# Attention scores: the second product of a split matmul reads k's low part where it was written, against a zero-padded copy of q's high part

## The chip, the cores and the metric

The kernel runs on one core of a Trainium2 chip. The metric is device time in microseconds (us): the time of one execution from launch to end. The core's engines are TensorE (PE: matmuls, and PEld for its weight loads), VectorE (DVE), ScalarE (ACT), GpSimd (POOL) and SyncE (SP), which here only issues transfers (DMA). Each engine runs its own list of instructions in order; semaphores hold an instruction until what it needs is there. Matmul results go to PSUM, and VectorE or ScalarE must read them out before that PSUM buffer can be used again.

## The reference, cut to what matters

Three stages follow one another on inputs of batch 4 and sequence 768: a linear attention over 8 heads, a gated feed-forward layer, and a causal softmax attention over 4 "experts" with head size 64. Only the last one is touched:

```python
for e in range(E):                      # E = 4
    q = x @ wq[e]                       # [768, 384] @ [384, 64]
    k = x @ wk[e]
    v = x @ wv[e]
    scores = scale * (q @ k.transpose(0, 2, 1))
    scores = np.where(causal, -1000000000.0, scores)
    scores = scores - scores.max(-1, keepdims=True)
    a = np.exp(scores)
    a /= a.sum(-1, keepdims=True) + 1e-09
    ye = a @ v @ wo[e]
    ...                                 # weighted by the gate, summed into out
```

The weights wq and wk are large here, so the scores need more precision than one matmul in the short float format fp32r gives. Each of q and k is therefore kept as a high part (qh, kh, rounded to fp32r) and a low part (ql, kl, the rest).

## The kernel before

**Stages.** The linear attention and the feed-forward layer run interleaved in an order written out by hand until about 358 us of the span. The softmax attention follows, as class Attention. Its instructions are created by `run` in an interleaved order, and a list scheduler with a model of its own then sets each engine's order at build time; SyncE's transfers go through one queue in order.

**Pairs and units.** The attention works on 8 pairs of heads (2 for each of 4 batches), called pair 0 to pair 7 below. For each pair `qk_group` makes q and k for both heads at once (128 partitions, head 0 on partitions 0 to 63, head 1 on 64 to 127) in two halves of 384 columns: nine matmuls into a PSUM tile m, ScalarE writes the high part, VectorE writes the low part from m and the high part. The tiles m come from a pool of two buffers that `qk_group`, `v_group` (the values, nine matmuls of 260 columns each, six times per batch), `av` and `proj_out` share. `soft` makes scores for one head and one block of 128 rows of q (12 blocks per pair, 96 in all): two matmuls into a PSUM tile st (two buffers; for the two widest blocks two matmuls on each of two column halves, so 128 of each kind in all), then VectorE adds the mask and takes the row extreme (sm, mn), then ScalarE takes the exponential (A). `transp` scales A, transposes it in blocks of 128 and copies it to T; `av` multiplies by the values; `proj_out` projects and stores.

**The two products.** Both have all 128 partitions as the contraction, so a head's 64 rows are there twice. Tile sq holds qh of the head on its own 64 partitions and ql of the head on the other 64; tile sk holds kh on both. So the first product, sq with sk, is qh·kh + ql·kh. Tile sl holds kl on both halves, and the second product, sq with sl, is qh·kl + ql·kl. [...] The first product is called S1 and the second S2 below. In `soft` before:

```python
q = hl["sq"][j]
for i, k in enumerate((hl["sk"][j], hl["sl"][j])):
    nc.tensor.matmul(st[:, z, 0:n], q[:, qi * C:(qi + 1) * C], k[:, z * n:(z + 1) * n], start=(i == 0), stop=(i == 1))
```

**Where the two stages meet.** The attention's left pools (qh, ql, kh, kl, m and the weights) are open while the feed-forward stage still ends, so q and k of pair 0 are made there. The right pools (A, T, V, and the pool lp, which holds sl) take the memory that the feed-forward stage gives back, some of it only when the last weight (st_wo) has been split into its high and low parts by VectorE.

Of the kernel before, what the change touches and what calls it, by code (L numbers as in the profile page):

```python
# [47 lines left out]
DIAG_ON_ACT = 6  # L48
STEPS = (2, 1, 1, 1, 1, 1, 1, 1, 1, 1, 1, 1, 1, 0)
FROM = 8  # L50


def _f(ap):
# [852 lines left out]


class Attention:
    def __init__(self, tc, nc, a, x2, out, ident):
        self.tc, self.nc, self.a, self.x2, self.out, self.ident = tc, nc, a, x2, out, ident  # L910
        self.left, self.right = ExitStack(), ExitStack()
        self.flip, self.raw = True, {}

    def open_left(self):
        tc, nc, a = self.tc, self.nc, self.a
# [20 lines left out]
    def open_right(self):  # L936
        tc = self.tc
        R = lambda n, b, **k: self.right.enter_context(tc.tile_pool(name=n, bufs=b, side="right", **k))
        self.ap = R("ap", 2)
        self.sp = R("sp", 3)  # L940
        self.lp = R("lp", 2)
        self.ps_s = R("ps2_s", 2, space=PSUM)

    P3 = ((0, 0), (0, 1), (1, 0))
# [56 lines left out]
    def qk_group(self, xs, hl, n, p, h):  # L1001
        nc = self.nc
        w, sc = (self.wq, -0.125) if n == "q" else (self.wk, 1.0)
        if h == 0:
            hl[n] = [self.qp.tile([128, S], F32R, name=n + z, bufs=1) for z in "hl"]
        hi, lo = hl[n]
        s = slice(h * HT, (h + 1) * HT)
        pt = self.ps_m.tile([128, 512], F32, name="m")
        m = 0
        for i in range(3):  # L1010
            for wi, xi in self.P3:
                self.shown = nc.tensor.matmul(pt[:, 0:HT], w[wi][:, i, p * 128:(p + 1) * 128], xs[xi][:, i, s],
                                              start=(m == 0), stop=(m == 8))
                m += 1
        nc.scalar.activation(hi[:, s], pt[:, 0:HT], AF.Copy, scale=sc)
        nc.vector.scalar_tensor_tensor(lo[:, s], pt[:, 0:HT], sc, _f(hi[:, s]), op0=OP.mult, op1=OP.subtract)
        if h == 0:
            return
        ts = []
        for j in range(2):  # L1020
            o, z = slice(64 * j, 64 * j + 64), slice(64 - 64 * j, 128 - 64 * j)
            t = self.qp.tile([128, S], F32R, name=f"s{n}{j}")
            nc.sync.dma_start(_f(t[o]), _f(hi[o]))
            nc.sync.dma_start(_f(t[z]), _f((lo if n == "q" else hi)[o]))
            ts.append(t)
        hl["s" + n] = ts
        if n == "k":
            hl["sl"] = []
            for j in range(2):
                o, z = slice(64 * j, 64 * j + 64), slice(64 - 64 * j, 128 - 64 * j)  # L1030
                t = self.lp.tile([128, S], F32R, name=f"sl{j}")
                nc.sync.dma_start(_f(t[o]), _f(lo[o]))
                nc.sync.dma_start(_f(t[z]), _f(lo[o]))
                hl["sl"].append(t)

    def v_group(self, xs, V, t):
        nc = self.nc
        pt = self.ps_m.tile([128, 512], F32, name="m")
        m = 0
        for i in range(3):  # L1040
            for xi, wi in self.P3:
                nc.tensor.matmul(pt[:, 0:260], xs[xi][:, i, t * C:(t + 1) * C], self.wv[wi][:, i],
                                 start=(m == 0), stop=(m == 8))
                m += 1
        if t in V_ON_DVE:
            nc.vector.tensor_copy(V[:, t], pt[:, 0:260])
        else:
            nc.scalar.activation(V[:, t], pt[:, 0:260], AF.Copy)
# [27 lines left out]
    def soft(self, hl, j, qi, A, rs):  # L1076

        nc, sp = self.nc, self.sp
        W = (qi + 1) * C
        nb = 1 if W <= 512 else 2  # L1080
        n = max(W, 256) // nb
        q = hl["sq"][j]
        st = self.ps_s.tile([128, 2, 512], F32, name="st")
        for z in range(nb):
            for i, k in enumerate((hl["sk"][j], hl["sl"][j])):
                nc.tensor.matmul(st[:, z, 0:n], q[:, qi * C:(qi + 1) * C], k[:, z * n:(z + 1) * n], start=(i == 0),  # L1086
                                 stop=(i == 1))
# [12 lines left out]
        nc.scalar.activation(at, o3, AF.Exp, bias=mn, scale=-1.0, accum_out=rs[:, qi % 3:qi % 3 + 1])  # L1100
# [7 lines left out]
    def transp(self, A, rs, T, qi):  # L1108
        nc = self.nc
        q = qi % 3  # L1110
        at = A[:, self.OFF[qi]:self.OFF[qi] + (qi + 1) * C]
        if self.unit >= SCALED_ON_POOL:
            nc.gpsimd.tensor_tensor(at, at, rs[:, q:q + 1].to_broadcast([128, (qi + 1) * C]), op=OP.mult)
        else:
            nc.vector.tensor_scalar(at, at, rs[:, q:q + 1], None, op0=OP.mult)
        for k0 in range(0, qi + 1, 4):
            k1 = min(qi + 1, k0 + 4)
            pt = self.ps_t.tile([128, 4, C], F32, name="t")
            for ki in range(k0, k1):
                nc.tensor.transpose(pt[:, ki - k0], at[:, ki * C:(ki + 1) * C], self.ident)  # L1120
            self.flip = not self.flip
            to = T[:, k0:k1, q * C:(q + 1) * C]
            if self.flip:
                nc.scalar.activation(to, pt[:, 0:k1 - k0], AF.Copy)  # L1124
            else:
                nc.vector.tensor_copy(to, pt[:, 0:k1 - k0])  # L1126

    def av(self, Ts, V, p, h, O):
        nc = self.nc
        po = self.ps_m.tile([128, 512], F32, name="m")  # L1130
        n = 3 * (h + 1)
        for ki in range(n):
            lo = max(0, ki - 3 * h) * C
            for j in range(2):
                o = slice(64 * j, 64 * j + 64)
                nc.tensor.matmul(po[o, lo:HT], V[:, ki, (2 * p + j) * 64:(2 * p + j + 1) * 64], Ts[j][:, ki, lo:],  # L1136
                                 start=(ki == 0), stop=(ki == n - 1))
        s = slice(h * HT, (h + 1) * HT)
        nc.scalar.activation(O[0][:, p, s], po[:, 0:HT], AF.Copy)
        nc.vector.tensor_tensor(O[1][:, p, s], po[:, 0:HT], _f(O[0][:, p, s]), op=OP.subtract)  # L1140

    def proj_out(self, b, O, t):
# [2 lines left out]
        m = 0  # L1145
        for p in range(2):
            for oi, wi in self.P3:
                nc.tensor.matmul(pt[:, 0:DM], O[oi][:, p, t * C:(t + 1) * C], self.wo[wi][:, p], start=(m == 0),  # L1148
                                 stop=(m == 5))
# [8 lines left out]
    def run(self):  # L1158
# [26 lines left out]
        def softs(j):  # L1185
# [3 lines left out]
            for e in range(2):  # L1189
                for q in range(3):  # L1190
                    def f(e=e, q=q):
                        if q == 0:
                            A = ap.tile([128, (6, 15)[h] * C], F32, name=f"A{h}", bufs=3)
                            rs = sp.tile([128, 3], F32, name="rs", bufs=6)
                            st[j].append((A, rs))
                        if j % 4 == 1 and (e, q) == (1, 0):
                            with self.tc.issue_after(self.shown.ins):
                                self.soft(HL[i], e, 3 * h + q, *st[j][e])
                        else:
# [4 lines left out]
        def tail(j):  # L1204
# [4 lines left out]
            for e in range(2):  # L1209
                for q in range(3):  # L1210
                    def f(e=e, q=q):
# [5 lines left out]
                        self.transp(A, rs, Ts[e], 3 * h + q)  # L1217
                    todo.append(f)

            def g():  # L1220
                if b not in OS:
                    OS[b] = [ap.tile([128, 2, S], F32R, name=f"O{z}", bufs=1) for z in range(2)]
                self.av(Ts, VS[b], p, h, OS[b])
            todo.append(g)
            half[b, h] = half.get((b, h), 0) + 1
            if half[b, h] == 2:
                for t in range(3):
                    todo.append(lambda t=t: self.proj_out(b, OS[b], 3 * h + t))
            return todo

        st, half = {}, {}
# [35 lines left out]
def stages(tc, nc, a, x2, out, ident, stat, lim, top):  # L1267

    right = ExitStack()
    at = Attention(tc, nc, a, x2, out, ident)  # L1270
    mi = []

    def left2():
# [100 lines left out]
```

## Time and profile before

| what | value |
|---|---|
| median of 3 runs | 597.36 us (596.36 to 597.47) |
| the profiled execution: its time, its span from first to last instruction | 596.38 us, 594.7 us |
| share of the span that PE, DVE, ACT, POOL are busy | 95%, 83%, 67%, 29% |
| mean granted clock of TensorE over the span | 0.976 |
| the attention's stretch, 357.8 us to the end: PE busy | 225.4 of 236.9 us |

How to read it: a busy share is an average over stages with different limits. A matmul's record covers its way through the array, which overlaps the next matmul's start, so the start of one to the start of the next is shorter than a record (18 matmuls of 384 columns with records of about 0.345 us stand in 3.35 us), and a PE that waits shows less idle time than it lost: about 0.17 us less for each wait. A granted clock of 1.00 is 2.4 GHz, of 0.50 is 1.2 GHz.

### The profile page before, as it was taken

The numbers are of one execution on the slowest core, as the hardware profiler recorded it, in microseconds if no ns is written. First come the engines' busy times: TensorE is split into PE (matmuls) and PEld (weight loads), VectorE is DVE, ScalarE is ACT, GpSimd is POOL, SyncE is SP. The second block draws the span as 40 slices with busy tenths as digits, with TensorE's granted clock in tenths as the row PEclk, the third lists the DMA queues.
The fourth block names the chain that finished last, engine by engine and source line by source line (L and its number), as shares of the span: only waits on it lengthen the run. The fifth ranks groups of instructions, "written<-read, shape, count | busy, mean of one in ns | idle before, by whom it ended". The sixth has DMA issues, their size and how long they took to land. (4 is left out here: it accounts for less than half of the span.)

```text
span 594.7 us, 12388 instructions
## 1 busy us (share of the span) xinstructions
PE 563.1 (95%) x4386; PEld 507.1 (85%) x4386; DVE 493.5 (83%) x1153; ACT 398.0 (67%) x1015; POOL 173.3 (29%) x246
## 2 busy tenths in 40 slices
PE   4788989999999999999999999999999999999986
PEld 4676888999999999989999999697979788978754
DVE  6999999999999999999967774988768667884741
ACT  4986657767778788887775765765666565654632
POOL 3666562335344342425310000400030021002440
PEclk9868889999999999999999999999999999999999
DMA  7676524664747868775453326760376153606202
GB/s 238 229 254 197 176 78 132 200 171 127 215 131 212 289 226 257 236 219 181 121 161 99 120 57 168 215 156 6 107 213 146 38 122 96 159 27 152 63 1 86
DMA packets 47158, 90.41 MB, mean 152 GB/s; under 512 B 14320, under 2 KB 28656, under 8 KB 47088
## 3 DMA queue, kind: packets, MB, share of 16 engines
q1 hardware_dynamic: 47088, 89.53, 51.2%
q8 instruction: 37, 0.61, 0.4%
q14 instruction: 33, 0.27, 0.2%
HBM read 50.23 MB, written 9.44 MB: 100 GB/s over the span
## 5 line engine op out<-in xcount | busy, mean ns | idle before, releaser
L447 PE MATMUL hs<-X,win 128*128 128x384 f32 (+1 forms) x576 | 118.1, 349 | 1.0 <-ACT ht L451 1.0
L447 PEld LDWEIGHTS hs<-X,win 128*128 128x128 f32 x576 | 98.9, 189 | 3.9 <-ACT ht L451 1.7
L521 PE MATMUL x<-gh,wout 128*128 128x386 f32 (+1 forms) x384 | 100.3, 343 | 0.0
L1099 DVE CUSTOM_DVE_ANT_0 sm<-st,mask 128x128 f32<-128x128 f32 (+5 forms) x96 | 58.6, 618 | 26.7 <-PE st L1086 23.4
L484 ACT ACTIVATE st<-ct 128x382 f32<-128x382 f32 (+1 forms) x64 | 33.7, 527 | 68.7 <-DVE ct L479 35.4
L1100 ACT ACTIVATE A<-sm,mn 128x128 f32<-128x128 f32 (+5 forms) x96 | 63.7, 664 | 20.1 <-DVE mn L1099 19.1
L302 POOL TENSOR_SCALAR_AFFINE_SELECT AT<-e 128x384 f32<-128x384 f32 x52 | 43.6, 859 | 108.9 <-DVE e L292 107.7
L521 PEld LDWEIGHTS x<-gh,wout 128*128 128x128 f32 x384 | 71.7, 193 | 0.0
L521 PE MATMUL x<-gl,wout 128*128 128x382 f32 (+1 forms) x192 | 65.8, 343 | 0.0
L1120 PE MATMUL t<-ident,A 128*128 128x128 f32 x336 | 51.7, 275 | 1.9 <-ACT T L1124 0.8
L1120 PEld LDWEIGHTS t<-ident,A 128*128 128x128 f32 x336 | 39.8, 140 | 8.0 <-issue 2.6
L1086 PE MATMUL st<-sk,sq 128*128 128x384 f32 (+3 forms) x128 | 44.2, 352 | 0.9 <-DVE mn L1099 0.6
L1136 PE MATMUL m<-T,V 128*64 128x384 f32 (+2 forms) x288 | 44.2, 422 | 0.3 <-ACT T L1124 0.3
L1086 PE MATMUL st<-sl,sq 128*128 128x384 f32 (+3 forms) x128 | 41.0, 328 | 2.8 <-DMA sl<-kl 2.8
L1126 DVE COPY T<-t 128x128 f32<-128x128 f32 (+3 forms) x64 | 32.2, 503 | 13.0 <-PE t L1120 12.2
L493 DVE SCALAR_TENSOR_TENSOR st<-st,ht 128x382 f32<-128x382 f32 (+1 forms) x64 | 36.4, 568 | 7.1 <-ACT st L484 5.4
L258 DVE TENSOR_TENSOR_SCAN Dp<-wkr,cD 128x387 f32<-128x387 f32 x32 | 39.1, 1221 | 3.6 <-POOL cD L174 3.6
L455 ACT ACTIVATE ct<-ht,cwk 128x382 f32<-128x382 f32 (+1 forms) x64 | 39.5, 618 | 2.1
L1124 ACT ACTIVATE T<-t 128x512 f32<-128x512 f32 (+3 forms) x64 | 28.5, 446 | 17.3 <-PE t L1120 17.0
L310 ACT ACTIVATE Fp<-wkr,lim 128x384 f32<-128x384 f32 x64 | 38.8, 607 | 0.3
L1136 PEld LDWEIGHTS m<-T,V 128*64 128x64 f32 x288 | 20.8, 136 | 20.0 <-issue 14.4
L319 PE MATMUL sc<-Q,K 64*128 64x128 f32 x384 | 35.2, 314 | 2.2 <-DVE AT L325 2.2
(148 smaller groups left out, 1313.8 us busy)
## 6 DMA issues: line engine op xcount, KB each, us to landing
wkr<-in_wkr SPq DMA_DIRECT2D x25, 578.0 KB, 4.1
v<-in_rkv SPq DMA_DIRECT2D x32, 192.0 KB, 3.9
rawt<-in_win SPq DMA_DIRECT2D x8, 768.0 KB, 5.6
rawt<-in_wout SPq DMA_DIRECT2D x8, 768.0 KB, 5.6
sk<-kh SPq DMA_DIRECT2D x32, 192.0 KB, 3.4
sl<-kl SPq DMA_DIRECT2D x32, 192.0 KB, 4.0
rn<-in_rkv SPq DMA_DIRECT2D x20, 288.0 KB, 3.6
x<-x SPq DMA_DIRECT2D x12, 384.0 KB, 4.5
```

The costliest lines, as they stand in the source:

```text
L258: nc.vector.tensor_tensor_scan(fl(t["Dp"]), t["w"][:, 0:NW], fl(cD), 0.0, op0=OP.mult, op1=OP.add)
L302: nc.gpsimd.affine_select(AT[:, j], t["e"][:, j][:, :, None].to_broadcast([128, CH, C]), pattern=[[0, CH], [1, C]], compare_op=OP.is_equal ...
L310: nc.scalar.activation(Fp[:, :, 0:C], wc, AF.Relu, bias=lim[:, z:z + 1], scale=(-1.0, 1.0)[z], accum_out=stat[:, 2 * u + z:2 * u + z + 1])
L447: nc.tensor.matmul(hs[:, 0:N], win[wi][:, f // 2, i, (f % 2) * 128:(f % 2 + 1) * 128], x[:, i, xi], start=(n == 0), stop=(n == 8))
L455: nc.scalar.activation(ct, ht[:, o:o + N], AF.Copy, scale=w[:, 1, f:f + 1])
L493: nc.vector.scalar_tensor_tensor(st, st, 1.0, ht[:, o:o + N], op0=OP.add, op1=OP.mult)
L521: nc.tensor.matmul(acc[0][i][:, 0:N], wout[wi][:, f, i * 128:(i + 1) * 128], G[g][gi], start=(f == 0 and z == 0), stop=(f == NF - 1 and z ...
L1086: nc.tensor.matmul(st[:, z, 0:n], q[:, qi * C:(qi + 1) * C], k[:, z * n:(z + 1) * n], start=(i == 0), stop=(i == 1))
L1099: nc.vector.tensor_tensor_reduce(o3, i3, m3, 1.0, 3e38, op0=OP.add, op1=OP.min, accum_out=mn)
L1100: nc.scalar.activation(at, o3, AF.Exp, bias=mn, scale=-1.0, accum_out=rs[:, qi % 3:qi % 3 + 1])
L1120: nc.tensor.transpose(pt[:, ki - k0], at[:, ki * C:(ki + 1) * C], self.ident)
L1136: nc.tensor.matmul(po[o, lo:HT], V[:, ki, (2 * p + j) * 64:(2 * p + j + 1) * 64], Ts[j][:, ki, lo:], start=(ki == 0), stop=(ki == n - 1))
```

## The change

- `soft`: S2 is now the product of zq and kl. Tile zq of a head holds qh of that head on its own 64 partitions and zero on the other 64, so it can be multiplied with kl as it lies there, both heads' rows at once: qh·kl of one head. The term ql·kl is left out.
- sl and its four transfers for each pair are gone. zq takes two transfers for each pair, issued where q is finished; 10 transfers for each pair stand in place of 12, 80 in place of 96.
- Two sets of zq (names zq0 and zq1 with the head's number behind) are used in turn; pair 0 takes set 1. Their zero halves are written once: in `open_right` by four memsets of 64 partitions x 768, two on GpSimd (set 0) and two on VectorE (set 1).
- kl moves from the left pool qp (one buffer) to the right pool lp (two buffers), where zq lies as well.
- `behind` and `PINS` only write the one existing exception of the order in another form: block (1, 0) of units 1, 5, 9, 13 is issued behind the last matmul of `qk_group`, as before. `last` keeps the handles for it.

```diff
-        self.lp = R("lp", 2)
+        self.lp = R("lp", 1)
+        self.zq = [[self.lp.tile([128, S], F32R, name=f"zq{z}{j}") for j in range(2)] for z in range(2)]
+        for z, e in zip(self.zq, (tc.nc.gpsimd, tc.nc.vector)):
+            for j, t in enumerate(z):
+                e.memset(_f(t[64 - 64 * j:128 - 64 * j]), 0.0)
...
-            hl[n] = [self.qp.tile([128, S], F32R, name=n + z, bufs=1) for z in "hl"]
+            hl[n] = [(self.lp if n + z == "kl" else self.qp).tile([128, S], F32R, name=n + z,
+                                                                  bufs=2 if n + z == "kl" else 1) for z in "hl"]
...
-        if n == "k":
-            hl["sl"] = []
-            for j in range(2):
-                o, z = slice(64 * j, 64 * j + 64), slice(64 - 64 * j, 128 - 64 * j)
-                t = self.lp.tile([128, S], F32R, name=f"sl{j}")
-                nc.sync.dma_start(_f(t[o]), _f(lo[o]))
-                nc.sync.dma_start(_f(t[z]), _f(lo[o]))
-                hl["sl"].append(t)
+        if n == "q":
+            self.zq.reverse()
+            hl["zq"] = self.zq[0]
+            for j, t in enumerate(self.zq[0]):
+                o = slice(64 * j, 64 * j + 64)
+                nc.sync.dma_start(_f(t[o]), _f(hi[o]))
...
-        q = hl["sq"][j]
+        q, k, c = hl["sq"][j], hl["sk"][j], slice(qi * C, (qi + 1) * C)
         st = self.ps_s.tile([128, 2, 512], F32, name="st")
         for z in range(nb):
-            for i, k in enumerate((hl["sk"][j], hl["sl"][j])):
-                nc.tensor.matmul(st[:, z, 0:n], q[:, qi * C:(qi + 1) * C], k[:, z * n:(z + 1) * n], start=(i == 0),
-                                 stop=(i == 1))
+            e = slice(z * n, (z + 1) * n)
+            nc.tensor.matmul(st[:, z, 0:n], q[:, c], k[:, e], start=True, stop=False)
+            self.last["st"] = nc.tensor.matmul(st[:, z, 0:n], hl["zq"][j][:, c], hl["k"][1][:, e], start=False,
+                                               stop=True)
```

The scheduler orders the attention anew. Three places show what moves.

VectorE where the stages meet, before: the low part kl of pair 0 (line 1016) is written between the two halves of the last weight's split (line 966).

```order
L966 TENSOR_TENSOR wv_4444<-st_wv,wv_4443 128x260 x2
L966 TENSOR_TENSOR wo_4446<-st_wo,wo_4445 128x384
L1016 SCALAR_TENSOR_TENSOR kl<-m,kh 128x384 x2
L966 TENSOR_TENSOR wo_4446<-st_wo,wo_4445 128x384
L1046 COPY V<-m 128x260
```

The same place now (the changed kernel's lines 978, 1029 and 1057 are 966, 1016 and 1046 of before; zq_4862 and zq_4863 are set 1 for head 0 and head 1):

```order
L978 TENSOR_TENSOR wv_4444<-st_wv,wv_4443 128x260 x2
L978 TENSOR_TENSOR wo_4446<-st_wo,wo_4445 128x384 x2
L953 MEMSET zq_4862 64x768
L953 MEMSET zq_4863 64x768
L1029 SCALAR_TENSOR_TENSOR kl<-m,kh 128x384 x2
L1057 COPY V<-m 128x260
```

Both writes of kl, which read the two m tiles of pair 0's k, moved behind the second half of the split and behind both memsets.

TensorE from the last matmul of the feed-forward stage on, now (line 522 is 521 of before; 1053 is v_group, line 1042 of before; 1097 is S1, 1098 is S2; sk_4932 and sq_4898 are head 0 of pair 0):

```order
L522 MATMUL x_4643<-gl,wout_154 128x386
L1097 MATMUL st<-sk_4932,sq_4898 128x256 x2
L1053 MATMUL m<-wv_4443,xs_4471 128x260
L1053 MATMUL m<-wv_4444,xs_4471 128x260
L1053 MATMUL m<-wv_4443,xs_4472 128x260
```

Before, two groups of `v_group` (18 matmuls of 260 columns) stood between that last matmul and these S1, and four groups (36 matmuls) between the S1 and their S2. Now the S1 come first, then two groups, then the S2 (line 1098), and the other four groups stand between later scores.

TensorE at the change from pair 0 to pair 1, now: from the last matmul of k for pair 1 (line 1025, 1012 of before) to the first score of pair 1 (sk_5127); line 1132 is a transpose, 1120 of before.

```order
L1025 MATMUL m<-xs_4471,wk_4442 128x384
L1097 MATMUL st<-sk_4935,sq_4901 128x512
L1098 MATMUL st<-kl,zq_4863 128x512
L1132 MATMUL t<-ident,A_5035 128x128 x3
L1097 MATMUL st<-sk_4935,sq_4901 128x320
L1098 MATMUL st<-kl,zq_4863 128x320
L1097 MATMUL st<-sk_4935,sq_4901 128x320
L1098 MATMUL st<-kl,zq_4863 128x320
L1097 MATMUL st<-sk_4935,sq_4901 128x384
L1098 MATMUL st<-kl,zq_4863 128x384
L1097 MATMUL st<-sk_4935,sq_4901 128x384
L1098 MATMUL st<-kl,zq_4863 128x384
```

Four more transposes of 128 columns follow, and then S1 of pair 1. Before, 39 matmuls and transposes stood there in place of these 17, among them the nine of the next q's first half and one pair of scores more.

## Rows read from the trace of the kernel before

**Rows 1.** The page: span, busy share of each engine, TensorE's clock in 40 slices.
```profile
span 594.7 us, 12388 instructions
PE 563.1 (95%) x4386; PEld 507.1 (85%) x4386; DVE 493.5 (83%) x1153; ACT 398.0 (67%) x1015; POOL 173.3 (29%) x246
...
PEclk9868889999999999999999999999999999999999
```

**Rows 2.** Waits from 357 us on: us in total, times, longest.
```profile
DVE sm L1099 <- PE st L1086: 23.4, 26, 4.5
...
PE st L1086 <- DMA sl<-kl: 2.8, 4, 1.0
```

**Rows 3.** TensorE's timeline at pair 3: start, length, [idle before].
```profile
435.33 0.60 PE L1148 MATMUL m<-wo,O 128*128 128x384 f32 x2
436.63 0.35 PE L1086 MATMUL st<-sl,sq 128*128 128x256 f32 x1 [0.70 <-DMA sl<-kl]
```

**Rows 4.** TensorE's timeline where the stages meet.
```profile
357.86 2.36 PE L1042 MATMUL m<-wv,xs 128*128 128x260 f32 x18
360.06 0.40 PE L1086 MATMUL st<-sk,sq 128*128 128x256 f32 x2
...
364.70 0.48 PE L1086 MATMUL st<-sl,sq 128*128 128x256 f32 x2
```

**Rows 5.** VectorE's timeline at the same place.
```profile
355.27 1.01 DVE L1016 SCALAR_TENSOR_TENSOR kl<-m,kh 128x384 fp32r<-128x384 f32 x2
359.00 0.56 DVE L966 TENSOR_TENSOR wo<-st_wo,wo 128x384 fp32r<-128x384 f32 x1 [2.72 <-ACT wo L963]
...
365.21 0.29 DVE L1099 CUSTOM_DVE_ANT_0 sm<-st,mask 128x128 f32<-128x128 f32 x1 [4.53 <-PE st L1086]
```

**Rows 6.** Nearest to a memset of 768 columns on VectorE: POOL's timeline, VectorE by form.
```profile
313.87 0.74 POOL L929 MEMSET mask<- 128x768 f32 x1 [10.90 <-PE m L405]
...
L1099 DVE CUSTOM_DVE_ANT_0 sm<-st,mask 128x768 f32<-128x768 f32 x16 | 15.2, 952 | 3.7 <-PE st L1086 3.3 <-ACT A L1100 0.2
...
L1115 DVE TENSOR_SCALAR A<-A,rs 128x768 f32<-128x768 f32 x12 | 7.4, 613 | 0.0
```

**Rows 7.** SyncE's timeline: issues for pairs 0 and 1; then landing times of tile sk.
```profile
356.09 0.60 SPq L1024 DMA_DIRECT2D sk<-kh  x1
...
359.62 0.46 SPq L1032 DMA_DIRECT2D sl<-kl  x1
...
373.76 0.60 SPq L1024 DMA_DIRECT2D sk<-kh  x1
...
DMA to landing us min/median/max: 2.5/3.4/3.9
```

**Rows 8.** TensorE's timeline in pair 1: the last k, and two waits.
```profile
370.95 1.75 PE L1012 MATMUL m<-xs,wk 128*128 128x384 f32 x9
...
380.54 0.44 PE L1120 MATMUL t<-ident,A 128*128 128x128 f32 x2 [0.36 <-DVE A L1115]
...
381.61 0.39 PE L1086 MATMUL st<-sk,sq 128*128 128x256 f32 x1 [0.29 <-DVE mn L1099]
```

**Rows 9.** Windows: us, busy of PE, PEld, DVE, ACT, POOL; granted clock, DMA.
```profile
55.00:60.00 5.00, 2.72 (x17) 2.31 (x17) 5.00 (x9) 4.42 (x12) 1.33 (x2) 1.00 0.76 242
...
80.00:85.00 5.00, 4.71 (x22) 4.65 (x23) 5.00 (x10) 3.71 (x11) 0.00 (x0) 0.69 0.10 33
...
370.00:380.00 10.00, 9.64 (x52) 7.81 (x51) 9.29 (x29) 8.23 (x21) 5.96 (x9) 1.00 0.89 211
380.00:390.00 10.00, 9.13 (x54) 7.07 (x54) 9.90 (x35) 6.71 (x20) 0.33 (x1) 1.00 0.68 193
```

**Rows 10.** TensorE's timeline in the first stage, two long idle times.
```profile
58.72 0.44 PE L334 MATMUL m<-ident,K 128*128 128x128 f32 x2 [2.01 <-DVE gl L508]
...
80.29 0.32 PE L368 MATMUL m<-Ss,ident 128*64 128x48 f32 x4 [1.69 <-ACT Ss L362]
```

**Rows 11.** TensorE's timeline near the end.
```profile
574.55 0.85 PE L1120 MATMUL t<-ident,A 128*128 128x128 f32 x6 [0.46 <-POOLq L1306]
```

More of the change, by code (lines that the diff above doesn't have):

```diff
@@ L50 @@
 FROM = 8
+PINS = {(1, "st", 1, 0): "qk"}
 def _f(ap):
@@ L908, with __init__, behind @@
 class Attention:
-    def __init__(self, tc, nc, a, x2, out, ident):
+    def __init__(self, tc, nc, a, x2, out, ident, fast=False):
+        self.fast = fast
         self.tc, self.nc, self.a, self.x2, self.out, self.ident = tc, nc, a, x2, out, ident
         self.left, self.right = ExitStack(), ExitStack()
-        self.flip, self.raw = True, {}
+        self.flip, self.raw, self.last = True, {}, {}
+    def behind(self, j, what, e=0, q=0):
+        p = PINS.get((j % 4, what, e, q))
+        if self.fast and p in self.last:
+            return self.tc.issue_after(self.last[p].ins)
+        return ExitStack()
     def open_left(self):
@@ L1011, in qk_group @@
             for wi, xi in self.P3:
-                self.shown = nc.tensor.matmul(pt[:, 0:HT], w[wi][:, i, p * 128:(p + 1) * 128], xs[xi][:, i, s],
-                                              start=(m == 0), stop=(m == 8))
+                self.last["qk"] = nc.tensor.matmul(pt[:, 0:HT], w[wi][:, i, p * 128:(p + 1) * 128], xs[xi][:, i, s],
+                                                   start=(m == 0), stop=(m == 8))
                 m += 1
@@ L1041, in v_group @@
             for xi, wi in self.P3:
-                nc.tensor.matmul(pt[:, 0:260], xs[xi][:, i, t * C:(t + 1) * C], self.wv[wi][:, i],
-                                 start=(m == 0), stop=(m == 8))
+                self.last["v"] = nc.tensor.matmul(pt[:, 0:260], xs[xi][:, i, t * C:(t + 1) * C], self.wv[wi][:, i],
+                                                  start=(m == 0), stop=(m == 8))
                 m += 1
@@ L1119, in transp @@
             for ki in range(k0, k1):
-                nc.tensor.transpose(pt[:, ki - k0], at[:, ki * C:(ki + 1) * C], self.ident)
+                self.last["t"] = nc.tensor.transpose(pt[:, ki - k0], at[:, ki * C:(ki + 1) * C], self.ident)
             self.flip = not self.flip
@@ L1135, in av @@
                 o = slice(64 * j, 64 * j + 64)
-                nc.tensor.matmul(po[o, lo:HT], V[:, ki, (2 * p + j) * 64:(2 * p + j + 1) * 64], Ts[j][:, ki, lo:],
-                                 start=(ki == 0), stop=(ki == n - 1))
+                self.last["av"] = nc.tensor.matmul(po[o, lo:HT], V[:, ki, (2 * p + j) * 64:(2 * p + j + 1) * 64],
+                                                   Ts[j][:, ki, lo:], start=(ki == 0), stop=(ki == n - 1))
         s = slice(h * HT, (h + 1) * HT)
@@ L1147, in proj_out @@
             for oi, wi in self.P3:
-                nc.tensor.matmul(pt[:, 0:DM], O[oi][:, p, t * C:(t + 1) * C], self.wo[wi][:, p], start=(m == 0),
-                                 stop=(m == 5))
+                self.last["o"] = nc.tensor.matmul(pt[:, 0:DM], O[oi][:, p, t * C:(t + 1) * C], self.wo[wi][:, p],
+                                                  start=(m == 0), stop=(m == 5))
                 m += 1
@@ L1195, in f @@
                             st[j].append((A, rs))
[L1196 to L1199, printed above, removed]
+                        with self.behind(j, "st", e, q):
                             self.soft(HL[i], e, 3 * h + q, *st[j][e])
@@ L1216, in f @@
                         self.unit = j
-                        self.transp(A, rs, Ts[e], 3 * h + q)
+                        with self.behind(j, "t", e, q):
+                            self.transp(A, rs, Ts[e], 3 * h + q)
                     todo.append(f)
@@ L1222, in g @@
                     OS[b] = [ap.tile([128, 2, S], F32R, name=f"O{z}", bufs=1) for z in range(2)]
-                self.av(Ts, VS[b], p, h, OS[b])
+                with self.behind(j, "av"):
+                    self.av(Ts, VS[b], p, h, OS[b])
             todo.append(g)
@@ L1226, in tail, with out @@
             if half[b, h] == 2:
+                def out(t):
+                    with self.behind(j, "o", 0, t):
+                        self.proj_out(b, OS[b], 3 * h + t)
                 for t in range(3):
-                    todo.append(lambda t=t: self.proj_out(b, OS[b], 3 * h + t))
+                    todo.append(lambda t=t: out(t))
             return todo
@@ L1269, in stages @@
     right = ExitStack()
-    at = Attention(tc, nc, a, x2, out, ident)
+    at = Attention(tc, nc, a, x2, out, ident, True)
     mi = []
```

## The prediction

> **What bounds the kernel now.** The page comes first: TensorE is busy 95% of the span, no other engine over 83%, and its clock is granted to 90% or more in every slice from the seventh on [rows 1]. The attention is the last stage and its TensorE order has few holes, so the list of waits tells what can be won there: only one kind of wait carries the name of the removed transfer, S2 waiting for sl, 4 times and 2.8 us of idle time; VectorE's 23.4 us of waiting for scores shows which engine is ahead of which [rows 2]. One of the four stands in the timeline of pair 3: two matmuls of `proj_out` start at 435.33, and S2 only at 436.63, after 0.70 us of idle [rows 3]. The others are like it, at pairs 4, 5 and 7. A wait costs about 0.17 us more than the idle shown, since the record before it covers what the next matmul would have overlapped, so the four cost 2.8 + 4 x 0.17 = 3.5 us.
>
> **S2 itself.** The shapes and the number of S2 are the same, the weights are another tile of 128 x 128: nothing on TensorE. The 32 transfers of sl leave SyncE's queue and 16 of zq come in, ahead of sk instead of behind it. The first thing that a pair's scores now need last is sk: S2 needs kl, which VectorE writes before SyncE is through with sk, and zq, which is issued before sk. So the 3.5 us go, **-3.5 us**. Bounds: -2.8 (the idle alone) and -3.5. What would be late next at those places is sk; the order gives pairs 3, 5 and 7 the same work between k and S1 as before, where S1 did not wait, so I take nothing for it.
>
> **Where the stages meet.** This is what the change adds. Before, kl of pair 0 was written at 355.27, and `v_group` began at 357.86 with no hole [rows 4, 5]. Now both writes of kl stand on VectorE behind the second half of the weight's split, which ScalarE releases at 359.00 and which ends at 359.56 [rows 5], and behind two memsets. Queued behind kl is TensorE: the two m buffers hold pair 0's k until kl has read them, and the first group of `v_group` needs one of the two. Its price: VectorE runs no memset in this trace. The nearest row is GpSimd's memset of 128 x 768, 0.74 us; VectorE's own rows of 768 columns bound it, 0.613 us for a scaling in SBUF and 0.952 us for the masking [rows 6]. I take 0.74 as the same operation, and half of the two kl (1.01 us, so about 0.55 with the end) for the first of them. `v_group` starts at 359.56 + 2 x 0.74 + 0.55 = 361.6, between 361.3 and 362.0 by the bounds. The S1 that now come first take 0.24 us (512 columns at the 2.2 us for 4680 of `v_group` [rows 4]); their sk lands at 356.09 + 3.4 = 359.5 [rows 7], inside the hole. Without a hole `v_group` would start at 357.86 + 0.24 = 358.1. So TensorE loses 361.6 - 358.1 = **+3.5 us** (3.2 to 3.9).
>
> The Trainium skill ("VectorE: DVE Perf Modes", section on zero memsets issued as uint32) says that a memset takes one cycle per element whatever the type, which at that page's 0.96 GHz is an estimated 0.80 us for 768 elements; by it this term would be 0.1 us larger. No run so far shows a memset on VectorE.
>
> The S2 behind these two groups waits for zq of set 1. Its transfer takes the place of sl's first, issued at 359.62; at 3.4 us (3.9 at most) it lands at 363.0 to 363.5 [rows 7]. `v_group` needs 2.2 us for two groups (357.86 to 360.06 [rows 4]), until 363.8, and hides it. If that cover fails by the length of a memset it costs half a microsecond. The two memsets on GpSimd, busy 29%, are needed a pair later: nothing.
>
> **The clock.** The hole is larger than any in the attention before. In the first stage idle times of this size brought TensorE to its lower level: 1.69 us of idle before 80.29, then a mean granted clock of 0.69 in the window 80 to 85, that is, most of 3 us at 1.2 GHz [rows 9, 10]. Idle of 2.01 us before 58.72 left the window 55 to 60 at 1.00 [rows 9, 10]. In the window 80 to 85 the clock lacks 0.31 x 5 us = 1.55 us of full speed: **+1.5 us**. Bounds: 0, if it stays, and 3, if it lasts twice as long. I take the fall, since here some 3.5 us hold only two matmuls.
>
> The Trainium skill ("TensorE: Matmul & The Clock Gate", section on why this matters for your kernels) warns of idle gaps between bursts of matmuls, which put the clock back to half. [...]
>
> **VectorE's backlog.** From 365.21 on, when the first scores arrive after 4.53 us of waiting [rows 5], VectorE runs without a pause and holds TensorE up: 9.90 us busy of the 10 after 380 [rows 9], with TensorE waiting for it at 380.54 and 381.61 [rows 8]. TensorE is idle 0.36 us of the ten to 380 and 0.87 us of the ten to 390 [rows 9], in some six waits, so with 0.17 us more for each it loses 2.2 us. Now the first scores come at 363.8 instead of 364.7, while TensorE's other work comes 3.5 us later, so VectorE has some 4 us more room for the same 12 blocks of pair 0. I take the loss as gone: **-2.2 us** (-1 to -2.2).
>
> **Pair 1's first score.** The order now leaves 17 matmuls and transposes between k and S1 of pair 1. They stream 2 x 512 + 4 x 320 + 4 x 384 + 7 x 128 = 4736 columns; `v_group` needs 2.2 us for 18 x 260 = 4680 columns [rows 4], so these need 2.2 us, and some 2.4 with the narrow ones. Before, k ended at 370.95 + 1.75 = 372.70, the second transfer of head 0's sk was issued at 373.76, and at 3.4 us it landed 4.5 us after k's end [rows 7, 8]; the 39 instructions covered that. Now 4.5 - 2.4 = 2.1 us are bare, of which VectorE's pace in that stretch would take a little anyway: **+1.8 us** (0 to 2.3).
>
> **The sum.** -3.5 + 3.5 + 1.5 - 2.2 + 1.8 = +1.1 us. Against the profiled execution's 596.38 us (span 594.7 and 1.7 around it) that is 597.5. That execution is among the fastest of those shown; against their median of 597.36 it is 598.5. I forecast 598.0. The end of the kernel, where transposes wait for the scaling on GpSimd [rows 11], gets scores earlier by the new order; I count nothing for it, with 0.5 us either way. Differences under 0.2%, 1.2 us, can't be told from none in this kernel.
>
> **Rivals.**
> First, *no change of note*, the sum as it stands: what the four waits give is paid where the stages meet. For it: every term has its row. 597 to 598.5, chance 0.42.
>
> Second, *faster*: the clock keeps its level through the hole (as after 58.72 at first), or pair 1's S1 is covered because VectorE paces TensorE there anyway. Without the clock's fall the sum is -0.4, which could not be told from none; without pair 1's wait too it is -2.2, and with the end's 0.5 us -2.7: 594.7 to 595.2 for the median. It decides whether the hole, broken by two matmuls at about 359.5, is short enough on either side. Against it: 1.69 us sufficed at 80.29. Chance 0.28.
>
> Third, *slower*: the clock falls a second time in pair 1. The place is the wait of S1 for sk, 1.8 us of idle after the last transposes, as long as the idle before 80.29 that was followed by a fall; the price is another 1.5 us, or the first fall lasts twice as long. Sum +2.6, 599.0 to 600.0. It decides at about 1.7 us of idle. Against it: VectorE, near its limit there, would hide part. Chance 0.30.
>
> That the change doesn't remove what it says is not among them: the issue order shows no transfer of sl. That its cost at the meeting of the stages is zero is excluded by the order of VectorE alone: kl can't start before 359.56.
>
> **Chances.** Same 0.42, faster 0.28, slower 0.30. The range reaches from the second rival's low end to a little beyond the third's: 594.9 to 600.6. The likeliest case's own range is 597.0 to 599.0.
>
> **What would show it.** Right: no wait for sl; in VectorE's timeline two memsets of 0.6 to 0.95 us behind the split of the weight, and kl behind them; `v_group` starting at 361.3 to 362.0 after a wait for kl; a granted clock below 1.00 in a stretch of about 3 us near 362; S1 of pair 1 waiting 1 to 2 us for sk; fewer waits for VectorE before 390. Wrong: `v_group` starts before 360.5, or the clock stays at 1.00, or S2 waits for kl or zq at the later pairs as it did for sl, which would take back the 3.5 us.

## The result, and the profile after

The kernel after takes 601.37 us (median of 6 runs, 600.88 to 602.60) against 597.41 us (596.36 to 599.27) for the kernel before on the same chip: ratio 1.007, 95% interval 1.0058 to 1.0082, so 3.5 to 4.9 us slower. The forecast was 598.0 us with a range up to 600.6; the time lies 0.8 us above it. The third rival (slower, by a second fall of the clock) named the direction; its price, up to 600.0, was too small too.

The profiled execution took 601.28 us. Its page, to be read beside [rows 1]:

```profile
span 599.6 us, 12352 instructions
...
PE 567.9 (95%) x4386; PEld 511.5 (85%) x4386; DVE 495.6 (83%) x1155; ACT 397.6 (66%) x1015; POOL 175.4 (29%) x248
...
PEclk9759889999999999999999998899999999999999
```

TensorE's shares and counts are the same; VectorE and GpSimd have two instructions more each (the fills). New are two eights in the row of the clock, in the 25th and 26th slice: 360 to 390 us.

The list of waits from 357 us on (us in total, times, longest), which answers to [rows 2]:

```profile
DVE sm L1111 <- PE st L1098: 13.9, 25, 1.8
...
PE m L1053 <- DVE kl L1029: 1.9, 1, 1.9
PE st L1097 <- issue: 1.9, 2, 1.3
PE st L1097 <- DMA sk<-kh: 1.5, 1, 1.5
```

The four waits of S2 for sl are gone, and no S2 waits for kl or zq in their place. Three rows are new: `v_group` waits for kl, and S1 (L1097) waits three times. The two filed under "issue" are waits for sk as well: the S1 of pair 1 starts at 383.94, and the second transfer of its sk lands at 383.74.

TensorE where the stages meet, to set against [rows 4]:

```profile
357.23 0.34 PE L522 MATMUL x<-gl,wout 128*128 128x386 f32 x1
359.03 0.47 PE L1097 MATMUL st<-sk,sq 128*128 128x256 f32 x2 [1.46 <-DMA sk<-kh]
361.45 3.94 PE L1053 MATMUL m<-wv,xs 128*128 128x260 f32 x18 [1.95 <-DVE kl L1029]
365.23 0.40 PE L1098 MATMUL st<-kl,zq 128*128 128x256 f32 x2
```

VectorE there, to set against [rows 5]:

```profile
358.54 0.56 DVE L978 TENSOR_TENSOR wo<-st_wo,wo 128x384 fp32r<-128x384 f32 x1 [3.65 <-ACT wo L975]
359.39 0.70 DVE L953 MEMSET zq<- 64x768 f32 x1 [0.29 <-DVE wo L978]
360.28 0.70 DVE L953 MEMSET zq<- 64x768 f32 x1 [0.20 <-issue]
360.90 0.95 DVE L1029 SCALAR_TENSOR_TENSOR kl<-m,kh 128x384 fp32r<-128x384 f32 x2
```

The first stage's last matmul starts at 357.23. Then TensorE has 1.46 us of nothing, two S1, and 1.95 us of nothing more until the first half of kl has freed an m buffer. The 18 matmuls of `v_group` then take 3.78 us to the next start, for which the kernel before took 2.20 [rows 4].

TensorE in pair 1, to set against [rows 8]:

```profile
377.50 1.73 PE L1025 MATMUL m<-xs,wk 128*128 128x384 f32 x9
...
382.28 0.33 PE L1132 MATMUL t<-ident,A 128*128 128x128 f32 x1 [0.35 <-ACT T L1136]
383.94 0.36 PE L1097 MATMUL st<-sk,sq 128*128 128x256 f32 x1 [1.33 <-issue]
```

Windows of the same execution (us, busy of PE, PEld, DVE, ACT, POOL, granted clock, DMA's share, GB/s); the two of ten us answer to [rows 9]:

```profile
360.00:365.00 5.00, 3.55 (x17) 3.56 (x18) 1.66 (x4) 0.39 (x1) 0.73 (x1) 0.66 0.57 188
...
385.00:390.00 5.00, 5.00 (x22) 4.42 (x20) 4.18 (x14) 1.61 (x5) 1.84 (x3) 0.66 0.74 213
...
370.00:380.00 10.00, 10.00 (x60) 9.54 (x58) 8.66 (x40) 5.80 (x16) 0.20 (x1) 1.00 0.40 99
380.00:390.00 10.00, 8.32 (x39) 6.87 (x38) 8.53 (x24) 6.61 (x16) 6.26 (x9) 0.83 0.87 216
```

The clock falls twice, each time behind idle time: 0.66 in the windows 360 to 365 and 385 to 390, where the kernel before had 1.00:

```profile
360.00:365.00 5.00, 5.00 (x42) 4.94 (x42) 0.43 (x1) 1.30 (x4) 0.00 (x0) 1.00 0.94 278
385.00:390.00 5.00, 5.00 (x35) 4.27 (x34) 4.92 (x18) 3.02 (x10) 0.00 (x0) 1.00 0.45 100
```

Each of the two windows after lacks 0.34 x 5 = 1.7 us of full speed.

Pair 3, where the kernel before waited for sl [rows 3], now has this:

```profile
439.76 0.49 PE L1132 MATMUL t<-ident,A 128*128 128x128 f32 x3
440.85 0.36 PE L1097 MATMUL st<-sk,sq 128*128 128x256 f32 x1 [0.60 <-issue]
```

It is S1 and not S2 that waits, and for sk: the tile's row of landing times in the window 425 to 440 says why, against 3.0/3.4/3.8 in the same window of the kernel before:

```profile
DMA to landing us min/median/max: 4.7/5.1/5.5
```

### The profile page after: what moved, and what is told of

The parts are those of the page before. It is cut to its first block, busy times and chain, and to the rows that moved or that the text cites. A ratio compares the mean times of both kernels' runs of the same rounds, so it can differ in the third digit from the quotient of the medians.

```text
span 599.6 us, 12352 instructions
## 1 busy us (share of the span) xinstructions
PE 567.9 (95%) x4386; PEld 511.5 (85%) x4386; DVE 495.6 (83%) x1155; ACT 397.6 (66%) x1015; POOL 175.4 (29%) x248
## 4 chain that ended last, share of the span: by engine, by line
PE 59%; DVE 21%; ACT 8%; DMA 5%; issue 3%; POOL 1%; SPq 1%; POOLq 0%; ACTq 0%; DVEq 0%
PE m L1025 9%; PE x L522 8%; PE hs L448 8%; PE m L1148 7%; PE t L1132 6%; PE m L1053 5%; PE m L1160 4%; PE st L1097 4%; PE st L1098 3%; DVE Dp L259 3%; DVE Fp L267 2%; PE sc L320 2%; DMA rawt<-in_wout 2%; DVE AT L326 2%; DVE ct L470 2%
## 5 line engine op out<-in xcount | busy, mean ns | idle before, releaser
L1132 PE MATMUL t<-ident,A 128*128 128x128 f32 x336 | 54.8, 276 | 2.5 <-ACT T L1136 1.9
L1097 PE MATMUL st<-sk,sq 128*128 128x384 f32 (+3 forms) x128 | 46.1, 365 | 3.5 <-issue 1.9
L1098 PE MATMUL st<-kl,zq 128*128 128x384 f32 (+3 forms) x128 | 41.2, 326 | 0.0
L509 DVE TENSOR_TENSOR gl<-st,gh 128x382 fp32r<-128x382 f32 (+1 forms) x64 | 35.6, 556 | 1.8 <-ACT gh L501 1.6
```

The costliest lines, as they stand in the source:

```text
L1097: nc.tensor.matmul(st[:, z, 0:n], q[:, c], k[:, e], start=True, stop=False)
L1098: self.last["st"] = nc.tensor.matmul(st[:, z, 0:n], hl["zq"][j][:, c], hl["k"][1][:, e], start=False, stop=True)
L1132: self.last["t"] = nc.tensor.transpose(pt[:, ki - k0], at[:, ki * C:(ki + 1) * C], self.ident)
```

## The experiments

Two causes were in question: the late start of the attention (kl behind the memory and the fills, with what follows of it), and losses spread over the stage. All kernels compute the whole reference. The last column is the span less the start of the first stage's last matmul, read from the profiled execution: it leaves out how the first stage went, whose last matmul starts between 357.18 and 359.60 in these profiles.

| kernel | median us | ratio to before, 95% interval | attention us |
|---|---|---|---|
| before | 597.41 | | 237.0 |
| after | 601.37 | 1.0070 (1.0058 to 1.0082) | 242.4 |
| e1 kl early | 593.67 | 0.9947 (0.9929 to 0.9965) | 234.1 |
| e2 fills on GpSimd | 599.95 | 1.0047 (1.0030 to 1.0064) | 239.3 |
| e3 pair 1 covered | 600.32 | 1.0056 (1.0039 to 1.0073) | 240.1 |
| e4 before, kl late | 605.14 | 1.0130 (1.0114 to 1.0147) | 247.3 |
| e5 after, second profile | 602.07 (one run) | | 240.7 |
| e6 four fills on VectorE | 605.15 | 1.0140 (1.0115 to 1.0164) | 245.9 |
| e7 e1, sk by two queues | 598.12 | 1.0021 (1.0005 to 1.0037) | 237.4 |
| e8 e1, pair 1 covered | 595.47 | 0.9980 (0.9965 to 0.9996) | 234.9 |
| e9 e1, zq by copy | 594.52 | 0.9953 (0.9937 to 0.9969) | 234.2 |
| e10 e1, fills on GpSimd | 593.06 | 0.9941 (0.9920 to 0.9963) | 233.9 |

**e1: the late start taken away.**

```diff
-hl[n] = [(self.lp if n + z == "kl" else self.qp).tile([128, S], F32R, name=n + z,
-                                                      bufs=2 if n + z == "kl" else 1) for z in "hl"]
+hl[n] = [(self.lp if n + z == "kl" and p else self.qp).tile([128, S], F32R, name=n + z, bufs=1) for z in "hl"]
```

> The kernel after, with kl of a batch's first pair taken from the pool that is open before the feed-forward ends (qp) and kl of its second pair from lp, so that pair 0's kl needs no memory that the wo split gives back; the four zero fills stay as they are. Theory (the lost time is the start of the attention: v_group begins 3.8 us late and the clock falls at 361.6 for 1.6 us, then pair 1's wait for sk and a second fall for about 3.6): v_group follows the first stage at about 357.6 without a wait, the first fall is gone, -5.4 us or more, 593 to 596.5 us. Rival (the lost time is spread over the attention: the new second product, the zq transfers, another order): the start moves and little else, 600 us or more.

593.67 us, as the theory had it, and 3.2 to 3.5 us under the kernel before (by the ratio and by the medians). TensorE where the stages meet:

```profile
357.19 0.34 PE L522 MATMUL x<-gl,wout 128*128 128x386 f32 x1
357.36 2.35 PE L1052 MATMUL m<-wv,xs 128*128 128x260 f32 x18
359.56 0.40 PE L1096 MATMUL st<-sk,sq 128*128 128x256 f32 x2
```

Its windows at the two places:

```profile
360.00:365.00 5.00, 4.52 (x38) 4.31 (x37) 1.67 (x7) 1.63 (x6) 0.69 (x1) 1.00 0.56 186
...
385.00:390.00 5.00, 5.00 (x36) 4.93 (x35) 4.65 (x19) 3.23 (x10) 0.00 (x0) 1.00 0.32 79
```

No hole, and the clock stays at 1.00 in both windows. VectorE still runs its two fills, at 359.35 and 360.24, behind the split of the weight: kl was written ahead of them, at 354.76. The rival is out: without the late start the change of S2 is a gain.

**e2: the fills moved, the memory wait left.**

```diff
-for z, e in zip(self.zq, (tc.nc.gpsimd, tc.nc.vector)):
+for z, e in zip(self.zq, (tc.nc.gpsimd, tc.nc.gpsimd)):
```

> The kernel after, with all four zero fills on GpSimd, so that VectorE has none between the wo split and kl. Theory (the start is late mainly because kl's memory is behind the wo split, and less because of the fills): kl starts 0.3 to 1.0 us behind the wo split instead of 2.4, v_group at 359.8 to 360.6 instead of 361.45, -1.0 to -1.8 us, 599.5 to 600.5 us, and the clock still falls near 360 unless the gap becomes too short. Rival (the two VectorE fills are the cause): v_group's wait is under 0.5 us and the first fall is gone, 597 us or less.

599.95 us, in the theory's range. TensorE:

```profile
359.26 0.47 PE L1097 MATMUL st<-sk,sq 128*128 128x256 f32 x2 [1.48 <-DMA sk<-kh]
360.04 5.04 PE L1053 MATMUL m<-wv,xs 128*128 128x260 f32 x27 [0.31 <-DVE kl L1029]
```

Counted from the last matmul of the first stage (357.44 here), `v_group` starts after 2.60 us, against 4.22 in the kernel after: the two fills were 1.6 of the delay. The rest is the S1 ahead of it, which wait for sk, and kl's memory. The clock falls all the same (0.66 in the window 360 to 365).

**e6: twice the fills.**

```diff
-for z, e in zip(self.zq, (tc.nc.gpsimd, tc.nc.vector)):
+for z, e in zip(self.zq, (tc.nc.vector, tc.nc.vector)):
```

> The kernel after, with all four zero fills on VectorE: twice the suspected cost. Theory (each fill stands between the wo split and kl and v_group waits for kl): kl starts 1.7 us later than in the kernel after (two fills at 0.85 from start to start), v_group at about 363.1, +1.7 us against the kernel after (603.1 us), less what e2 showed of the other side (-1.6 us of start for two fills less). Rival (beyond the wait for the memory, the start is hidden by the score products now ahead of v_group): 601 to 602 us.

The start follows the theory: with the first stage's last matmul at 358.74, `v_group` begins 6.01 us later, 1.8 more than in the kernel after.

```profile
364.75 2.32 PE L1053 MATMUL m<-wv,xs 128*128 128x260 f32 x9 [3.73 <-DVE kl L1029]
...
388.97 0.36 PE L1097 MATMUL st<-sk,sq 128*128 128x256 f32 x1 [2.28 <-DVE rs L1118]
```

The time does not: 605.15 us, 3.8 above the kernel after and 2 above the expectation. In the profiles the attention takes 3.4 us more (245.9 against 242.4). Of these 1.8 are the later start, and 0.9 stand in pair 1, where S1 now idles 2.28 us (its sk lands at 388.77). The rest, 0.5 to 0.7, lies at the hole, behind which the clock stays low for longer:

```profile
365.00:370.00 5.00, 5.00 (x26) 5.00 (x27) 1.23 (x6) 1.38 (x5) 0.00 (x0) 0.56 0.00 0
```

This window lacks 0.44 x 5 = 2.2 us; the kernel after lacks 1.7 behind its hole and has 1.00 here. The fall in pair 1 is as long as there (0.67 in the window 390 to 395). So a later start costs more than its own length, through pair 1 and through the clock.

**e4: the late start alone, in the kernel before.**

```diff
-hl[n] = [self.qp.tile([128, S], F32R, name=n + z, bufs=1) for z in "hl"]
+hl[n] = [(self.lp if n + z == "kl" else self.qp).tile([128, S], F32R, name=n + z, bufs=1) for z in "hl"]
...
 self.lp = R("lp", 2)
+t = self.lp.tile([128, S], F32, name="zero", bufs=1)
+for j in range(2):
+    tc.nc.vector.memset(t[64 - 64 * j:128 - 64 * j], 0.0)
```

> The kernel before, sl and its four transfers kept, with kl taken from lp (one buffer) and two zero fills of 64x768 on VectorE of a scratch tile that nothing reads: the start of the attention as the change makes it, alone. Theory: v_group is late by 3.8 us and the clock falls once there for 1.6 us, as in the kernel after; the waits for sl stay; +3 to +5.5 us, 600.5 to 603 us (the lower end if VectorE's stalls near 380 go as they did after). Rival (the late start is made up later, because VectorE and the transfers run ahead in it): within 1 us of before, 596.5 to 598.5 us.

605.14 us, 2 above the expected range. Its waits:

```profile
PE st L1089 <- DMA sl<-kl: 3.1, 4, 1.0
PE m L1045 <- DVE kl L1019: 1.9, 1, 1.9
PE st L1089 <- DMA sk<-kh: 1.5, 1, 1.5
PE st L1089 <- DVE rs L1107: 1.4, 1, 1.4
```

The hole is that of the kernel after (1.5 and 1.9 us), the waits for sl are back, and pair 1's S1 waits too (the row of 1.4 us; its sk lands at 384.67, it starts at 384.87). The clock falls at both places, and stays low for longer than in the kernel after:

```profile
360.00:365.00 5.00, 3.60 (x16) 3.60 (x17) 1.61 (x4) 0.39 (x1) 0.00 (x0) 0.56 0.68 186
365.00:370.00 5.00, 5.00 (x34) 5.00 (x33) 1.07 (x5) 1.65 (x6) 0.00 (x0) 0.76 0.28 79
380.00:385.00 5.00, 2.85 (x17) 2.22 (x15) 5.00 (x17) 4.60 (x10) 3.29 (x5) 0.94 0.67 154
385.00:390.00 5.00, 4.78 (x14) 2.97 (x15) 4.31 (x12) 1.98 (x5) 2.97 (x5) 0.50 0.99 238
390.00:395.00 5.00, 5.00 (x33) 4.22 (x32) 3.34 (x10) 2.12 (x6) 0.00 (x0) 0.87 0.45 173
```

The first two windows lack 0.44 x 5 + 0.24 x 5 = 3.4 us of full speed and the other three 0.06 x 5 + 0.50 x 5 + 0.13 x 5 = 3.4, twice the 1.7 of a fall in the kernel after, a little of it in idle time. The expectation had one fall of 1.6; what comes on top is more than its miss.

With e1 this makes a square of two changes: the new S2, and the late start with all that belongs to it (kl's memory, the two fills, the order that follows). The late start costs 1.3% without the new S2 (e4 to before) and 1.23% with it (1.0070 to 0.9947 of e1): 7.8 and 7.4 us. The new S2 gains 0.53% with kl early and 0.6% with kl late: 3.2 and 3.6 us. Each of these differences is known to about 1.3 us, by the intervals of the ratios, and within that the two parts add up. That they do so to 0.4 us is in part luck, since the profiles show that the clock's falls differ in length and number.

**e3: pair 1's wait covered, the start left.**

```diff
+FIRST = {(1, "st", 0, 1): "qk"}
...
-p = PINS.get((j % 4, what, e, q))
+p = PINS.get((j % 4, what, e, q)) or FIRST.get((j, what, e, q))
```

> The kernel after, with one order more: the first half's score rows of pair 0 from the second on (unit 1) stand behind the k projection of pair 1, so that about 1.4 us more work lies between that projection and pair 1's first score product. The start is left as it is. Theory (pair 1's first score product waits for sk 1.7 us and the clock falls behind that idle): the idle at 382 to 384 shrinks to under 0.5 us and the clock stays at 1.00 from 365 to 395, -2.5 to -3.6 us, 597.7 to 599 us. Rival A (the second fall comes of something else): the idle goes, the stretch at half clock near 385 stays, about 599.5 us. Rival B (the idle only moves to another place): 601 us.

600.32 us, above the theory's range. Waits of TensorE in pair 1:

```profile
381.88 0.41 PE L1098 MATMUL st<-sk,sq 128*128 128x320 f32 x1 [0.61 <-DVE mn L1112]
385.04 0.35 PE L1098 MATMUL st<-sk,sq 128*128 128x256 f32 x1 [1.16 <-DVE rs L1117]
```

The idle is split, not removed: 0.61 us now wait for VectorE at one of the delayed score rows, and 1.16 for sk (landed at 384.84). Rival B was right on the idle. Yet the clock stays at 1.00 from 380 to 395. That put a question to the second fall.

**e5: the kernel after, profiled again.**

> The kernel after, unchanged, profiled once more. Kernels e2 and e3 had 1.9 and 1.3 us of idle in one piece at the same place and no second stretch at half clock, so the idle alone may not decide it. Theory A (the second fall belongs to this program: idle of 1.3 us behind 0.35 us): the half clock begins again 1 to 2 us behind the first score product of pair 1, near 385.5. Theory B (it comes in some executions and not in others): no half clock between 365 and 590, and the time is about 1.5 us under that of the first profile, near 599.8 us, if the first stage takes the same.

The same program, and theory B on the clock. TensorE in pair 1:

```profile
386.37 0.35 PE L1097 MATMUL st<-sk,sq 128*128 128x256 f32 x1 [1.37 <-issue]
```

The window behind it:

```profile
390.00:395.00 5.00, 5.00 (x36) 4.25 (x35) 4.32 (x19) 3.91 (x12) 0.00 (x0) 1.00 0.31 88
```

1.37 us of idle and no fall, where the first profile had 1.33 and a fall. The attention took 240.7 us instead of 242.4: 1.7 us is the price of the second fall here, and an execution has it or not. The expected time of 599.8 us was wrong (602.07), since the first stage took 2.4 us more in this execution.

**e7 and e8: e1 with a change to sk's path or to pair 1's order.** e8's edit is that of e3 on e1; e7's is this, on e1:

```diff
-nc.sync.dma_start(_f(t[z]), _f((lo if n == "q" else hi)[o]))
+(nc.sync if n == "q" else nc.gpsimd).dma_start(_f(t[z]), _f((lo if n == "q" else hi)[o]))
```

> Kernel e1 (kl early) with the second of each two sk transfers issued by GpSimd's queue in place of SyncE's. Theory (after the change the first score product of a pair waits for sk, in pairs 3 and 5 for 0.43 and 0.84 us, in the place where the second one waited for sl): the second copy lands 0.5 to 0.9 us earlier, these waits shrink, -0.5 to -1.2 us against e1, 592.5 to 593.2 us. Rival (the transfer is slow for its own sake, or GpSimd's issue is late): 593.5 to 594.5 us.

> Kernel e1 (kl early) with the order of e3 (unit 1's score rows from the second on behind pair 1's k projection). Theory (in e1 the 1.16 us of idle near 376 is a transpose that waits for a copy on ScalarE behind three 768-column splits of x, not for sk): more work on TensorE between the two covers part of it, -0.3 to -1.0 us against e1, 592.7 to 593.4 us. Rival (the stall only moves behind the pinned rows, as in e3): 593.5 to 594.5 us.

Both expectations failed, and both times lie above the rivals' 594.5 too. In e7 the sk of pair 1 took this long:

```profile
DMA to landing us min/median/max: 4.0/4.4/5.1
```

In e1 the same window (370 to 384) has 3.4/3.9/4.3. By two queues the two transfers of a head land close together (379.31 and 379.40 for the first head), and the first of each head lands later: the rival's first half. (The Trainium skill, "DMA: Bandwidth & Descriptors", section on issuing engines not being separate DMA queues, says that starting transfers on several engines saves only the time to start them. The trace agrees: the four issues take 1.3 us instead of 2.6, and the last lands 5.8 us behind the first issue instead of 6.1.) 598.12 us, 4.4 worse than e1, and these runs don't show why. An S1 of pair 1 waits 1.17 us at 383.63, but for VectorE, 2.7 us after the pair's last sk landed (380.94); the waits for sk in pairs 3 and 5 are 0.63 and 0.21 us, in e1 0.26 and 0.67. In e8 the transpose's idle of 1.16 us is now 0.25 us in front of a transpose and 1.06 us in front of an S1; 595.47 us. Covering one wait in pair 1 moves it, as in e3.

**e9: zq without transfers.**

```diff
-nc.sync.dma_start(_f(t[o]), _f(hi[o]))
+nc.gpsimd.tensor_copy(t[o], _f(hi[o]))
```

> Kernel e1 (kl early) with zq's high rows written by two GpSimd copies of 64x768 for each pair, in place of two transfers. Theory (of the change, two zq transfers land ahead of sk in the same row of landings, 0.8 to 0.9 us apart, so that sk lands 4.3 us behind its issue where it landed 2.5 to 3.2 us behind it in the kernel before, and the first score product of pairs 3 and 5 waits for it): sk lands 1 to 1.7 us earlier against its k projection, the waits of 0.43 and 0.84 us in pairs 3 and 5 are gone, -0.8 to -1.5 us against e1, 592.2 to 592.9 us. Rival (GpSimd's copies are late, and the second product waits for zq in their place): 593.5 us or more.

The mechanism is shown, the time is not had. sk in the window 425 to 440:

```profile
DMA to landing us min/median/max: 2.9/3.1/3.6
```

That is about the value of the kernel before (3.4), against 5.0 in e1, and no S1 waits for sk any more (0.26 and 0.67 us in e1). But 594.52 us and 234.2 us of attention are e1's within the intervals. In pair 1 three waits of 0.24, 0.36 and 0.63 us for ScalarE and VectorE stand where e1 had one of 1.16; where the rest of the gain went is not shown. So zq's transfers cause the waits for sk, but no run shows that the kernel is faster without them.

**e10: the control to e2.** The edit of e2, on e1.

> Kernel e1 (kl early) with all four zero fills on GpSimd: the control to e2. Theory (the fills cost time only where kl stands behind them): 593.0 to 594.3 us, as e1. Rival (the fills on VectorE cost 1.4 us wherever they stand, as e2 against the kernel after): 592.3 us.

593.06 us; its interval and e1's overlap. The fills cost nothing that can be told where kl doesn't stand behind them.

## Why the prediction was wrong

Step by step, in microseconds; a stall is counted from start to start over the usual distance, as the prediction did.

| step | predicted | after, first profile | second profile (e5) |
|---|---|---|---|
| S2's waits for sl | -3.5 | -3.5 | -3.5 |
| S1's waits for sk in pairs 3 and 5 | 0 | +1.0 | +1.1 |
| hole where the stages meet | +3.5 | +3.8 | +3.7 |
| first fall of the clock | +1.5 | +1.6 | +1.6 |
| stalls of pairs 0 and 1, 374 to 390 | -2.2 + 1.8 | 0.0 | 0.0 |
| end of the kernel | 0 | +0.5 | +0.5 |
| second fall | a rival, +1.5 | +1.7 | 0 |
| sum | +1.1 | +5.1 | +3.4 |
| attention against before's 237.0 | | +5.4 | +3.7 |

**The removed wait.** Right: no wait names sl, and e4 to after and before to e1 give the new S2 a gain of 3.2 to 3.6 us. But the step said of sk, "I take nothing for it", since sk did not hold S1 up before. It took sk's landing from rows in which no zq stood ahead of it [rows 7]. With two zq transfers issued just before, sk landed after 5.1 us instead of 3.4 in pair 3, and S1 waits where S2 waited; e9 shows the cause by taking zq off the queue. So this term was wrongly put at nothing: the profile has +1.0 us of stalls. That they cost the kernel as much is not shown. e9 has none of them and is no faster than e1, and the 3.2 to 3.6 us that the new S2 gains as a whole, these stalls and the end's included, are what the prediction booked for it.

**Where the stages meet.** Mechanism right, size nearly: 3.7 to 3.8. The fills were taken as 0.74 us each; they last 0.70, but one starts 0.89 behind the other, and the first 0.29 behind the split, so kl starts 1.80 us behind the split's end (358.54 + 0.56) and not 1.48. No S2 of pair 0 waited for zq.

**The clock at the hole.** Right, +1.6 (3.78 us for 2.20). All six profiles with kl late show a fall, in e4 and e6 a longer one; e1 and its four relatives, without the hole, show none. (The Trainium skill, "TensorE: Matmul & The Clock Gate", section on why this matters for your kernels, says that a long idle gap between bursts of matmuls puts the clock back to half. For this hole, 1.46 and 1.95 us of idle with two matmuls between them, the traces agree; of the shorter gaps in pair 1, below, three of six were followed by a fall.) The row that spoke against a fall was read too short. Behind the idle before 58.72 the window 55 to 60 is at 1.00 [rows 9], but the next one of the kernel before is not:

```profile
60.00:65.00 5.00, 4.71 (x18) 4.65 (x18) 5.00 (x9) 1.50 (x5) 3.83 (x6) 0.66 0.35 125
```

So a fall followed both long idle times of [rows 10], and the second rival had no row for a clock that keeps its level.

**VectorE's backlog and pair 1.** Sk of pair 1 landed 4.5 us behind k's end (379.23 to 383.74), as worked out, and the S1 idled 1.33 us behind 0.35. The stalls that vanished (2.2) and those that came (2.3) cancel; predicted was -0.4. Booking the first as a gain of its own was a mistake of method: e3, e8 and e9 each remove a stall there and get it back at other instructions. (Between k and S1 of pair 1 the trace of the kernel before has 40 matmuls and transposes, not 39, and ten score matmuls more than the kernel after, not one pair.)

**The second fall.** It was rival three, with its place right, its price right in the kernel after (1.5; measured 1.7, but twice that in e4) and its condition wrong: "it decides at about 1.7 us of idle". The S1 of pair 1 idled 1.33 us in the first profile, 1.37 in e5, 1.16 in e3, 1.72 in e2, 1.38 in e4 and 2.28 in e6; the clock fell behind the first, fifth and sixth, and not behind e2's, longer than two of them. What decides, beside the length, these runs don't settle. It should have been priced into the main sum with a share, and added to, not weighed against, the rest.

**The end.** Transposes that wait for scaling and copies lost 3.4 us behind 562 us instead of 2.9; I had counted nothing, with 0.5 either way. It comes with the new S2 and not with the late start: e1 has the same last four waits as the kernel after (0.51, 0.56, 0.46 and 0.56 us of idle), e4 the same last three as the kernel before (0.20, 0.46 and 0.57; before 0.20, 0.46 and 0.56). Why the new S2 brings it stays open.

**The step that failed** is the price of the late start as a whole. The prediction gave it 4.6 us: 3.5 for the hole, 1.5 for the clock, and 1.8 - 2.2 for pairs 0 and 1. By the square of e1 and e4 it costs 7.4 to 7.8. Its parts in the profiles are 3.8 for the hole, 1.6 for the first fall and 0.0 for pairs 0 and 1, together 5.4, and 1.7 more where the second fall comes, together 7.1. So the gain of 0.4 in pairs 0 and 1 was not there, and the second fall, put at nothing in the sum, was, in some executions. What decides on it, and where the rest of the 7.4 to 7.8 lies, stays open. Every sign that the prediction named for being right was seen (`v_group` at 361.45, two fills of 0.70 us, S1 of pair 1 waiting 1.33 us), and the time still lay outside its range: the signs tested the terms in the sum and not those left out of it.

**A version that beats both** is e1 (or e10): the new S2 with kl of a batch's first pair in memory that is free before the feed-forward ends, 593.67 us, ratio 0.9947 to the kernel before.

## What to carry to other kernels

When a tile moves to another pool, ask when that memory becomes free, and who waits behind the first write to it: here a buffer's place, with two fills ahead of its first write, cost twice what the removed transfers gave. When a transfer is taken out of a queue and another put in at another place, take the landing times of what now stands behind the new one anew; rows from the old order don't hold. A gap at a stage's boundary costs more than its length, since the clock falls behind it and the next pair's transfers shift with it.

## What the runs showed of the chip that was not expected

VectorE's zero fill of 64 x 768 f32 lasts 0.70 us and is followed by the next after 0.89 (four in a row in e6: 360.90, 361.80, 362.69, 363.59). GpSimd needs 1.52 us for two and 3.06 us for four. The transfers of a pair land one behind the other: the ten of e1's pair 1, from sq to sk, within 8.3 us (372.06 to 380.32), and in e7, issued by two queues, within 7.9 us (373.04 to 380.94). What is issued last pays for what is ahead: without the two zq transfers sk landed after 3.1 us instead of 5.0 (e9, e1). A fall of the clock has no fixed price: it took 1.7 us of full speed in the kernel after, e2, e3 and e5, and 3.4 at each of two places in e4. And the same program, with the same idle time at the same place (1.33 and 1.37 us), lost its clock in one execution and kept it in the next.
